# Agent attention and a squared-ReLU FFN: a written order for every engine in the first batch's prologue

## The chip, the core and the metric

The kernel runs on one core of one Trainium2 chip. The metric is device time in microseconds (us); lower is better. The engines are PE (matrix multiplications), PEld (PE's weight loads), DVE (vector), ACT (scalar: activations and copies), POOL (GpSimd) and SP (here it only issues DMAs).

## What is computed

For each of 4 batches there are 12480 tokens of width 128 and 49 agents. In NumPy, with everything in float32 and the two FFN matrices handed over as float64 bits:

```
a2k     = softmax(scale * agents @ k.T)      # 49 x 12480, over the keys
agent_v = a2k @ v                            # 49 x 128
q2a     = softmax(scale * q @ agents.T)      # 12480 x 49, over the agents
x       = q2a @ agent_v                      # tokens x 128
h       = relu(x @ w_in)                     # tokens x 2048
y       = (h * h) @ w_out                    # tokens x 128
```

Since `x @ w_in` is `q2a @ (agent_v @ w_in)`, each batch needs a small table `agent_v @ w_in` (49 x 2048, kept as a high part `aw_hi`, a low part `aw_lo` and a half-precision remainder `aw_ex`), and the FFN multiplies the queries' weights with that table.

## The kernel before

A batch's tokens are cut into 13 blocks of 960; 52 blocks ("groups") of queries in all. The main loop, `first(k)` and `second(k)`, runs 416 pairs: matmuls of the query weights `w`, `x` with the table (tile `h`), a ReLU `r` and a square `g_hi` on ACT, products `gg`, `h` and remainders `g_lo` on DVE and POOL, and matmuls with `wo_hi`, `wo_lo` and `wo_half` into `o`. Keys, values and queries of later batches are slipped between those matmuls. Before the first pair can run, batch 0 needs a prologue, and the change is about that alone:

1. Keys. For each of 13 blocks, 8 matmuls give the scores (`scores`, L243), ACT copies them to `s` (L253), DVE folds them into a running maximum `mx` (L258).
2. `decode_w_in` (L136): `w_in` comes in 8 chunks of 256 columns (`raw`). Per chunk ACT takes the absolute value (L113), DVE clamps and shifts bits (L114, L118, L120, L127, L128), POOL adds the two parts into `win` (L139) and DVE reduces (L140).
3. `maxima` (L261): DVE reduces `mx` over the blocks (L264), PE transposes, DVE reduces again (L272), scales an identity (L274), PE spreads it, and `mb` (L282) holds the maximum of each agent.
4. Values. For each of 13 blocks DVE subtracts `mb` from the scores (L295, `weighed`), ACT takes the exponential (L309), and 8 matmuls (L326, `gathered`) add into the PSUM tile `psa`.
5. Query group 0 (`queries`): matmuls, maximum (L435), difference (L437), exponential, sum (L442), division on POOL (L445), halves (L288, L465).
6. `w_out` comes in 8 chunks too. `most_of_w_out` (L149), `magnitudes` (L114, L118, L120), `powers_of_w_out` (L151 to L171, with one matmul, L163), then `decode_w_out` (L173): DVE L176, L127, L128, ACT L179, L180, POOL L181, L182.
7. `tables` (L348): `x` (L352), matmuls with `quad`, `avT` and `mag` on ACT (L362, L364), a bound and powers of two on DVE, four matmuls with `win`, `aw_hi` on ACT (L402), `aw_lo` on DVE (L404), `aw_half` (L409) and DMAs on SP.

The engines' order here is made by a scheduler which takes what is ready; `issue_after` and `high_priority` push single pieces. So the order in the text of the program isn't the order on an engine. PSUM tiles come from `bank()`: three buffers in rotation (`ps_h`), the same three that the FFN's tiles `h` use.

Of the kernel before, what the change touches and what calls it, by code (L numbers as in the profile page):

```python
# [9 lines left out]
F32 = mybir.dt.float32  # L10
# [19 lines left out]
QAT = 1  # L30
FREE = 4
AFTER = 3
WARM0 = 16
PRE = 12
PAIRED = (0, 2, 4, 6, 1, 3, 5, 7)
OPEN = 10
HELD = 1
# [16 lines left out]
def agent_attention_relu2(ctx: ExitStack, tc: tile.TileContext, qT, kT, v, agT, w_in, w_out, outT):  # L54
# [48 lines left out]
    def load_raw(src):  # L103
        raw = dec.tile([P, WCH, 2], U32, name="raw", bufs=12)
# [4 lines left out]
    def magnitudes(raw, out):  # L109
        high = raw[:, :, 1]  # L110

        t = dec.tile([P, WCH], U32, name="t")
# [4 lines left out]

        nc.vector.tensor_scalar(t, t, 0x07FFFFFF, 3, op0=ALU.bitwise_and, op1=ALU.logical_shift_left)  # L118
        out = t if out is None else out
# [3 lines left out]
        return out  # L123

    def remainders(raw, t):
        rest = dec.tile([P, WCH], F32, name="rest")
        nc.vector.tensor_single_scalar(rest.bitcast(U32), t, 0xFF800000, op=ALU.bitwise_and)  # L127
        nc.vector.scalar_tensor_tensor(  # L128
            out=rest, in0=raw[:, :, 0], scalar=2.0**-52, in1=rest, op0=ALU.mult, op1=ALU.mult
        )  # L130
        return rest
# [4 lines left out]
    def decode_w_in(n, raw):  # L136
        cs = slice(n * WCH, (n + 1) * WCH)
        t = magnitudes(raw, None)
        nc.gpsimd.tensor_add(win[:, cs], t.bitcast(F32), remainders(raw, t))  # L139
        nc.vector.reduce_max(top[:, n : n + 1], win[:, cs], axis=AX.X, apply_absolute_value=True)  # L140

    def load_w_out(n):
        c = slice(n * WCH // C, (n + 1) * WCH // C)
        raw = load_raw(w_out.bitcast(U32).rearrange("(c p) d -> p c d", p=P)[:, c, :])
        return raw

    def most_of_w_out(raws):
        for n, raw in enumerate(raws):
            nc.vector.reduce_max(most_out[:, n : n + 1], raw[:, :, 1].bitcast(F32), axis=AX.X, apply_absolute_value=True)  # L149

    def powers_of_w_out():  # L151
# [10 lines left out]
        ps = ps_t.tile([P, 512], F32, name="o", tag="turn0")  # L162
        last[nc.tensor] = nc.tensor.matmul(ps[:, :1], ones, e.bitcast(F32), start=True, stop=True)  # L163
# [7 lines left out]
        return up.bitcast(F32), down.bitcast(F32)  # L171

    def decode_w_out(n, raw, up):  # L173
        c = slice(n * WCH // C, (n + 1) * WCH // C)
        t = raw[:, :, 1].bitcast(F32)
        nc.vector.tensor_scalar_mul(t, t, up)  # L176
        rest = remainders(raw, raw[:, :, 1])
        hi, lo, half = (x[:, c, :].rearrange("p c d -> p (c d)") for x in (wo_hi, wo_lo, wo_half))
        nc.scalar.copy(hi, t)  # L179
        nc.scalar.copy(half, t)  # L180
        nc.gpsimd.tensor_sub(t, t, hi.bitcast(F32))  # L181
        nc.gpsimd.tensor_add(lo, t, rest)  # L182
# [37 lines left out]
    def spin(n):  # L220
        if alone[0]:
            ps = bank()
            with tc.issue_after(last[nc.tensor].ins):
                for _ in range(n):
                    nc.tensor.matmul(ps[:, :P], ones, ones, start=True, stop=True)
# [35 lines left out]
    def maxima(b):  # L261
# [7 lines left out]
        spin(5)  # L269
# [9 lines left out]
        spin(6)  # L279
        yield 1  # L280
        st["mb"] = small.tile([TP, NA], F32, name="mb")
        st["below"] = nc.vector.tensor_copy(st["mb"], pb[:TP, :NA]).ins  # L282
# [7 lines left out]
    def weighed(b, i, vt, whole, eng):  # L290
        st = state[b]
        s = st["s"][i]
        mb = st["mb"].rearrange("p (o a) -> p o a", o=1).broadcast_to([TP, NT, NA])
        d = s if whole else small.tile([TP, NT, NA], F32, name="d", bufs=2)
        st["less"] = eng.tensor_sub(d, s, mb).ins  # L295
        R, W = (NA, C + 1) if whole else (K2, 2 * (C + 1))
        if not whole:
            vs = kv.tile([TP, NT, W], F32R, name="vs")
            nc.gpsimd.memset(vs.bitcast(F32)[:, :, C : C + 1], 1.0)
            nc.gpsimd.memset(vs.bitcast(F32)[:, :, 2 * C + 1 :], 0.0)  # L300
            nc.scalar.copy(vs[:, :, :C], vt[:, :, :C])
            yield PACE
            last[nc.gpsimd] = nc.gpsimd.tensor_sub(  # L303
                vs[:, :, C + 1 : 2 * C + 1], vt[:, :, :C], vs[:, :, :C].bitcast(F32)
            )
        else:
            nc.scalar.copy(vt[:, :, C:], ones[:TP, :NT].rearrange("p (t o) -> p t o", o=1))
        yield PACE
        nc.scalar.activation(d, d, AF.Exp, scale=scale)  # L309
        if whole:  # L310
            e = d
        else:
            e = small.tile([TP, NT, R], F32R, name="e2", bufs=2)
            yield from halves(e, d, NA, eng)
            vt = vs
        return e, vt, R, W, whole

    def gathered(b, i, e, vt, R, W, whole):
        st = state[b]
        if alone[0]:  # L320
            if i == 0:
                st["av"] = small.tile([K2, 2 * (C + 1)], F32, name="av")
                nc.gpsimd.memset(st["av"], 0.0)
                sums[0] = ps_t.tile([P, 512], F32, name="psa", tag="turn1")
            for t in range(NT):
                nc.tensor.matmul(  # L326
                    sums[0][:R, :W], e[:, t, :], vt[:, t, :],
                    start=(i == 0 and t == 0), stop=(i == NB - 1 and t == NT - 1),
                )
            if i == NB - 1:  # L330
                nc.vector.tensor_copy(st["av"][:NA, : C + 1], sums[0][:NA, : C + 1])
            return
        yield 0
        pv = bank()
        put([
            product(pv[:R, :W], e[:, t, :], vt[:, t, :], start=(t == 0), stop=(t == NT - 1)) for t in range(NT)
        ])
# [496 lines left out]
```

## Time and profile before

| | us |
|---|---|
| median of 3 runs | 1886.37 |
| lowest and highest run | 1885.26, 1886.77 |
| profiled execution, its own time | 1886.58 |
| its span | 1884.8 |
| PE busy | 1864.2 (99%) |
| DVE, ACT, POOL busy | 1646.2, 1667.8, 1334.9 |
| last matmul of the values starts (L326) | 59.93 |
| first matmul of the FFN (L511) | 77.56 |

Times in the trace are counted from the start of the span. PE is busy nearly throughout, except in the first 4% of the span: the page's 40 slices show PE at 9 and 7 tenths in the first two, and at 9 afterwards. A row of a view gives the engine, the line of the program, the tile that is written and the tiles that are read, the shape, and after "x" how many instructions the row holds.

### The profile page before, as it was taken

Reading aid. Unit: us, or ns where it says so; the run is one execution under the profiler, and the core shown is the slowest. Engines: PE = TensorE matmul, PEld = TensorE weight load, DVE = VectorE, ACT = ScalarE, POOL = GpSimd, SP = SyncE. Lnnn points to the kernel's source line nnn. Section 1 sums busy time; section 2 is a strip of 40 time slices with the busy share of each in tenths; the row PEclk is TensorE's granted clock in tenths of the full one; section 3 lists DMA queues with packets and bytes.
Section 4 is the critical chain, followed back from the end, with each engine's and each line's share of the span. In section 5 each row is a group of like instructions: output and inputs, shape, how many; then the busy total and the mean of one; then the engine's idle time right before and its main releaser. Section 6 shows DMA issues by size and latency. Waiting matters only on the chain.

```text
span 1884.8 us, 31149 instructions
## 1 busy us (share of the span) xinstructions
PE 1864.2 (99%) x10848; PEld 1419.0 (75%) x10848; DVE 1646.2 (87%) x1918; ACT 1667.8 (88%) x1607; POOL 1334.9 (71%) x1270
## 2 busy tenths in 40 slices
PE   9799999999999999999999999999999999999999
PEld 9578777777777777777777777777777777777776
DVE  5878888888998898888898888888899989899897
ACT  4578899999888899999888889999988999999997
POOL 1455788887666678888666568898866666767675
PEclk9799999999999999999999999999999999999999
DMA  9233223322112222322212212222112111111110
GB/s 372 75 113 95 80 73 96 93 82 85 54 63 68 84 67 90 95 77 95 78 46 63 81 51 74 82 74 81 58 42 64 41 54 51 52 53 48 52 37 28
DMA packets 74148, 144.53 MB, mean 77 GB/s; under 512 B 9356, under 2 KB 45864, under 8 KB 73992
## 3 DMA queue, kind: packets, MB, share of 16 engines
q1 hardware_dynamic: 73992, 142.55, 23.6%
q8 instruction: 86, 1.41, 0.3%
q14 instruction: 70, 0.57, 0.1%
HBM read 82.89 MB, written 25.56 MB: 58 GB/s over the span
## 4 chain that ended last, share of the span: by engine, by line
PE 93%; DVE 4%; ACT 1%; issue 1%; POOL 1%; POOLq 0%; DVEq 0%; ACTq 0%
PE o L511 56%; PE h L511 26%; PE psa L511 10%; PE h L214 1%; DVE gg L511 1%; ACT r L511 1%; ACT g_hi L511 0%; PE h L670 0%; DVE rest L127 0%; DVE s L295 0%; DVE mx L258 0%; DVE rest L128 0%; DVE g_lo L511 0%; DVE t L114 0%; POOL g_lo L542 0%
## 5 line engine op out<-in xcount | busy, mean ns | idle before, releaser
L542 POOL TENSOR_TENSOR g_lo<-gg,g_hi 128x480 f16<-128x480 f32 x832 | 997.1, 1220 | 454.5 <-ACT g_hi L511 252.9
L511 ACT ACTIVATE r<-h 128x960 f32<-128x960 f32 x832 | 763.6, 968 | 128.4 <-PE h L511 101.1
L511 ACT ACTIVATE g_hi<-r 128x1920 fp32r<-128x1920 f32 x416 | 754.9, 1815 | 26.8 <-POOL g_lo L542 0.4
L511 DVE TENSOR_TENSOR g_lo<-h,g_hi 128x960 f16<-128x960 f32 x416 | 480.0, 1154 | 121.2 <-ACT g_hi L511 93.3
L511 PE MATMUL o<-g_hi,wo_hi 128*128 128x480 f32 x1664 | 570.3, 424 | 0.0
L511 DVE TENSOR_TENSOR gg<-r,h 128x960 f32<-128x960 f32 x416 | 478.7, 1151 | 81.4 <-ACT r L511 72.6
L511 PE MATMUL o<-g_lo,wo_half 128*128 128x480 f16 x1664 | 517.0, 370 | 0.7 <-POOL g_lo L542 0.5
L511 PE MATMUL o<-g_hi,wo_lo 128*128 128x480 f32 x1664 | 496.9, 380 | 0.0
L511 DVE TENSOR_TENSOR h<-r,h 128x960 f32<-128x960 f32 x416 | 480.2, 1154 | 0.7
L511 PE MATMUL h<-w,aw_hi 128*128 128x480 f32 x1664 | 435.0, 383 | 4.5 <-DVE aw_lo L404 2.7
L511 PEld LDWEIGHTS h<-w,aw_hi 128*128 128x128 f32 x1664 | 311.8, 189 | 61.3 <-DVE gg L511 8.7
L511 PEld LDWEIGHTS o<-g_hi,wo_hi 128*128 128x128 f32 x1664 | 315.4, 190 | 48.6 <-issue 3.7
L511 PEld LDWEIGHTS o<-g_hi,wo_lo 128*128 128x128 f32 x1664 | 312.9, 188 | 49.2
L511 PEld LDWEIGHTS <-wo_half 128*128 128x128 f16 x1664 | 167.5, 115 | 124.6 <-issue 92.0
L511 PE MATMUL h<-x,aw_ex 19*128 19x480 f16 x1664 | 159.5, 373 | 0.0
L511 PEld LDWEIGHTS psa<-ag,qt 128*120 128x120 f32 x816 | 140.4, 187 | 18.7 <-DVE ob L511 4.7
L511 PE MATMUL psa<-ag,qt 128*120 128x49 f32 x816 | 126.3, 242 | 0.0
L511 PEld LDWEIGHTS <-aw_ex 19*128 19x128 f16 x1664 | 42.1, 91 | 106.3 <-issue 99.1
L511 PEld LDWEIGHTS psa<-ag,kt 128*120 128x120 f32 x624 | 93.5, 184 | 8.7 <-DVE ob L511 0.6
L511 PE MATMUL psa<-ag,kt 128*120 128x49 f32 x624 | 87.7, 249 | 0.0
L303 POOL TENSOR_TENSOR vs<-vt,vs 120x1024 fp32r<-120x1024 f32 x39 | 85.7, 2198 | 0.0
L511 DVE TENSOR_SCALAR ob<-o,down 128x480 f32<-128x480 f32 x104 | 72.3, 695 | 4.0 <-PE o L511 4.0
(147 smaller groups left out, 1039.6 us busy)
## 6 DMA issues: line engine op xcount, KB each, us to landing
qt<-in_qT SPq DMA_DIRECT2D x52, 480.0 KB
out_T<-ob SPq DMA_DIRECT2D x104, 240.0 KB
vt<-in_v SPq DMA_DIRECT2D x39, 516.0 KB
kt<-in_kT SPq DMA_DIRECT2D x39, 480.0 KB
w<-ph SPq DMA_DIRECT2D x102, 91.9 KB
w<-y SPq DMA_DIRECT2D x102, 91.9 KB
x<-half SPq DMA_DIRECT2D x416, 17.8 KB
ahead<-in_v SPq DMA_DIRECT2D x13, 516.0 KB
```

The lines of the kernel that those rows point to most:

```text
L214: last[nc.tensor] = nc.tensor.matmul(*args, **kw)
L303: last[nc.gpsimd] = nc.gpsimd.tensor_sub(vs[:, :, C + 1 : 2 * C + 1], vt[:, :, :C], vs[:, :, :C].bitcast(F32))
L511: ins = issue(*args, **kw)
L542: chain[nc.gpsimd] = nc.gpsimd.tensor_sub(lo[:, n, :], gg[:, n, :], hi[:, 0, n, :].bitcast(F32)).ins
```

## The change

The prologue is written out anew under `tc.manual_schedule()`: every engine runs its instructions in the order of the program's text. What differs in the work itself:

- The keys' DMAs alternate with those of `w_in`, and `w_in`'s chunks are decoded between the keys. Of a chunk's decode, the product of `rest` with the low word moves from DVE (L128) to ACT (a scaled copy, L135) and POOL (a multiplication, L138).
- The keys' softmax has two parts (`HALF = 7`): blocks 0 to 6 get the maximum `mb`, blocks 7 to 12 the running maximum `mb_late`. The values' sums lie in two PSUM tiles, `psa` and `o`; the first is scaled by `fall` = exp(early maximum less late maximum) when `x` is built (L756, L764).
- The 13 subtractions `s - mb` move from DVE (L295) to POOL (L704).
- One chunk of `w_out` is decoded on DVE behind each of eight blocks of values (L149, L108, L111, L112, L117, L119), and `powers_of_w_out` comes in the second last block; its matmul (L167) stands ahead of the last block's gather. What needs the power of two, `parts_of_w_out`, follows: three instructions on ACT, one on DVE, two on POOL per chunk, four chunks around `tables(0)` and four behind it.
- Two of the 16 small DMAs of the table go out from ACT's queue (L390); idle matmuls (`spin`, 2, 2, 1 and 8) stand between the steps of the table. `raw` has 10 buffers (12), `t` 3 (2).
- The last block of values is loaded twice (L747): 14 loads of values, 13 used.

```
-        t = magnitudes(raw, None)
-        nc.gpsimd.tensor_add(win[:, cs], t.bitcast(F32), remainders(raw, t))
+        t, rest = spare()
+        low = raw[:, :, 0]
+        magnitudes(raw, t, t)
+        nc.scalar.activation(low.bitcast(F32), low, AF.Copy, scale=2.0**-52)
+        nc.vector.tensor_single_scalar(rest, t, 0xFF800000, op=ALU.bitwise_and)
+        yield
+        nc.gpsimd.tensor_mul(low.bitcast(F32), low.bitcast(F32), rest.bitcast(F32))
+        nc.gpsimd.tensor_add(win[:, cs], t.bitcast(F32), raw[:, :, 0].bitcast(F32))
+        yield
         nc.vector.reduce_max(top[:, n : n + 1], win[:, cs], axis=AX.X, apply_absolute_value=True)
...
+        def weigh(i):
+            mb = mbs[i >= HALF].rearrange("p (o a) -> p o a", o=1).broadcast_to([TP, NT, NA])
+            d = st["s"][i]
+            nc.gpsimd.tensor_sub(d, d, mb)
+            nc.scalar.activation(d, d, AF.Exp, scale=scale)
+            nc.scalar.copy(vts[i][:, :, C:], ones[:TP, :NT].rearrange("p (t o) -> p t o", o=1))
...
         for i in range(NB):
+            key(i)
+            more(i)
+            if i == 8:
+                next(early)
+            if i == 10:
+                next(early)
+            if i == 11:
+                next(early, None)
+            for n, delay in ((i - 3, 0), (i - 4, 0), (i - 6, 0)):
+                if 0 <= n < NW:
+                    next(whole[n], None)
...
         for i in range(NB):
+            if i + 1 < NB:
+                weigh(i + 1)
+            gather(i)
+            if i == 0:
+                vts.append(load_values(0, NB - 1, pre, "ahead"))
+            if i < 3:
+                next(late, None)
+            if 1 <= i < NB - 2:
+                ahead_of(q0, 1)
+            n = i - 1 if i < 7 else i - 2
+            if 0 <= n < NW and i != 7:
+                decode_w_out(n, outs[n])
+            if i == HALF + 1:
+                nc.vector.tensor_scalar_mul(x[:NA, :], sums[0][:NA, : C + 1], fall)
+            if i == NB - 3:
+                next(powers)
+            if i == NB - 2:
+                run(powers)
         run(q0)
+        ahead = queries(1)
+        next(ahead)
+        nc.vector.tensor_add(x[:NA, :], x[:NA, :], sums[1][:NA, : C + 1])
+        for n in range(2):
+            parts_of_w_out(n, outs[n])
+        spin(2)
+        made = tables(0)
+        for at, _ in enumerate(made):
+            if at in (1, 3):
+                spin(2 - at // 2)
+            if at in (2, 4):
+                parts_of_w_out(1 + at // 2, outs[1 + at // 2])
+        spin(8)
+        for n in range(4, NW):
+            parts_of_w_out(n, outs[n])
```

DVE among the keys. Before, it had the running maximum of the blocks first (L258), and then two chunks of `w_in` mixed with one another:

```order
L256 COPY mx<-h 120x392
L258 TENSOR_TENSOR mx<-mx,h 120x392 x7
L114 TENSOR_SCALAR t<-t 128x256
L118 TENSOR_SCALAR t<-t 128x256
L114 TENSOR_SCALAR t<-t 128x256
L120 SCALAR_TENSOR_TENSOR t<-raw,t 128x256
L118 TENSOR_SCALAR t<-t 128x256
```

After the change, DVE in the midst of the keys (the late maximum's start, the reduction of the early one, and a chunk):

```order
L141 TENSOR_REDUCE top<-win 128x1
L679 TENSOR_TENSOR mx_late<-s,h 120x392
L683 TENSOR_REDUCE m_360<-mx 120x49
L108 TENSOR_SCALAR t<-t 128x256
L111 TENSOR_SCALAR t<-t 128x256
L112 SCALAR_TENSOR_TENSOR t<-raw,t 128x256
L136 TENSOR_SCALAR t<-t 128x256
```

All eight chunks of `w_in` now stand among the keys (four did before), one behind each maximum; L128 is gone from DVE.

POOL between the keys and the table, after the change (before, POOL had none of the subtractions here, only L139, L445, L288 and L465):

```order
L138 TENSOR_TENSOR raw<-raw,t 128x256
L139 TENSOR_TENSOR win<-t,raw 128x256
L704 TENSOR_TENSOR s<-s,mb 120x392
L740 MEMSET x 98x129
L704 TENSOR_TENSOR s<-s,mb 120x392 x3
L423 TENSOR_TENSOR e<-e,z 120x392
L704 TENSOR_TENSOR s<-s,mb 120x392 x2
L290 TENSOR_TENSOR pp<-e,pp 120x8x49
```

The subtraction of block 0 stands behind the last addition into `win`, and that of block 4 behind the queries' division L423.

PE at the end of the values, before:

```order
L326 MATMUL psa<-ahead,s 49x129 x38
L163 MATMUL o<-e_out,ones 128x1
L326 MATMUL psa<-ahead,s 49x129 x8
L214 MATMUL h<-quad,x 128x98
L214 MATMUL h<-x,quad 98x1
```

and after:

```order
L713 MATMUL o<-ahead,s 49x129 x24
L167 MATMUL h<-e_out,ones 128x1
L713 MATMUL o<-ahead,s 49x129 x8
L229 MATMUL h<-ones 128x128 x2
L219 MATMUL h<-quad,x 128x98
```

The matmul for the power of two stands ahead of the last gather in both. On DVE, the decode that it waits for was spread in pairs of chunks before; after the change each chunk is a row of dependent instructions, and after the powers comes `x` at once, with no decode between:

```order
L149 TENSOR_REDUCE most_out<-raw 128x1
L108 TENSOR_SCALAR t<-t 128x256
L111 TENSOR_SCALAR t<-t 128x256
L112 SCALAR_TENSOR_TENSOR raw<-raw,t 128x256
L117 TENSOR_SCALAR t<-raw 128x256
L119 SCALAR_TENSOR_TENSOR raw<-raw,t 128x256
L156 TENSOR_REDUCE v_out<-most_out 128x1
```

From the first pair of the FFN on, the order of all engines is that of before, but for the two copies of `tables` that changed places in batches 1 to 3.

## Rows read from the trace of the kernel before

**Rows 1.** The page: the span, and busy time of each engine.

```profile
span 1884.8 us, 31149 instructions
PE 1864.2 (99%) x10848; PEld 1419.0 (75%) x10848; DVE 1646.2 (87%) x1918; ACT 1667.8 (88%) x1607; POOL 1334.9 (71%) x1270
```

**Rows 2.** Busy time by stage: window, length, PE, PEld, DVE, ACT, POOL, PEclk, DMA, GB/s.

```profile
7.27:35.44 28.17, 26.79 (x250) 26.26 (x249) 17.05 (x45) 9.68 (x25) 3.02 (x4) 1.00 1.04 399
35.44:60.20 24.76, 24.71 (x218) 23.93 (x218) 23.83 (x80) 12.71 (x35) 6.09 (x8) 1.00 0.67 234
```

**Rows 3.** Timeline of PE: start, us, engine, line, out<-in, count [idle before <-releaser].

```profile
7.10 21.94 PE L214 MATMUL h<-ag,ahead 128*120 128x49 f32 x208
...
35.44 13.05 PE L326 MATMUL psa<-ahead,s 120*49 120x129 f32 x116 [0.28 <-ACT s L309]
...
58.23 1.97 PE L326 MATMUL psa<-ahead,s 120*49 120x129 f32 x16
63.80 0.46 PE L214 MATMUL h<-quad,x 98*128 98x98 f32 x2 [3.60 <-DVE x L352]
```

**Rows 4.** Groups by line and shape, 0 to 80 us, DVE: busy us, mean ns | idle before.

```profile
L258 DVE TENSOR_TENSOR mx<-mx,h 120x392 f32<-120x392 f32 x12 | 6.7, 561 | 7.8 <-ACT s L253 7.8
...
L120 DVE SCALAR_TENSOR_TENSOR t<-raw,t 128x256 uint32<-128x256 uint32 x8 | 3.2, 415 | 0.0
...
L127 DVE TENSOR_SCALAR rest<-t 128x256 uint32<-128x256 uint32 x8 | 2.2, 286 | 0.0
...
L264 DVE TENSOR_REDUCE m<-mx 120x49 f32<-120x392 f32 x1 | 0.8, 802 | 0.0
```

**Rows 5.** Every instruction of L295 in all batches: duration ns min/median/max.

```profile
L295 POOL TENSOR_TENSOR d<-s,mb x39: 943/962/979, 221.1 to 1346.9; 120x392 f32<-120x392 f32 x39
L295 DVE TENSOR_TENSOR s<-s,mb x13: 556/558/560, 34.3 to 40.9; 120x392 f32<-120x392 f32 x13
```

**Rows 6.** Groups by line and shape, 0 to 80 us, POOL and ACT.

```profile
L139 POOL TENSOR_TENSOR win<-t,rest 128x256 f32<-128x256 f32 x8 | 6.1, 763 | 29.1 <-DVE rest L128 29.1
...
L445 POOL TENSOR_TENSOR e<-e,z 120x392 f32<-120x392 f32 x1 | 0.8, 842 | 11.1 <-DVE z L444 11.1
...
L309 ACT ACTIVATE s<-s 120x392 f32<-120x392 f32 x13 | 6.4, 528 | 2.0 <-DVE s L295 2.0
...
L179 ACT CAST wo_hi<-raw 128x256 fp32r<-128x256 f32 x8 | 3.4, 427 | 1.1 <-DVE raw L176 1.1
```

**Rows 7.** Timelines around 26 us and around 46 us, DVE and POOL.

```profile
25.55 0.72 POOL L139 TENSOR_TENSOR win<-t,rest 128x256 f32<-128x256 f32 x1 [0.36 <-DVE rest L128]
...
25.73 0.70 DVE L114 TENSOR_SCALAR t<-t 128x256 f32<-128x256 f32 x1
...
26.46 0.29 DVE L118 TENSOR_SCALAR t<-t 128x256 uint32<-128x256 uint32 x1
...
46.06 1.00 POOL L288 TENSOR_TENSOR pp<-e,pp 120x392 fp32r<-120x392 f32 x1
...
46.17 0.41 DVE L140 TENSOR_REDUCE top<-win 128x1 f32<-128x256 f32 x1
...
46.50 0.71 DVE L118 TENSOR_SCALAR t<-t 128x256 uint32<-128x256 uint32 x1
```

**Rows 8.** Timelines of ACT and DVE from 66 us on.

```profile
72.09 0.69 ACT L402 ACTIVATE aw_hi<-h,rl 98x512 fp32r<-98x512 f32 x1 [6.07 <-DVE down L391]
...
94.77 1.83 ACT L511 ACTIVATE r<-h 128x960 f32<-128x960 f32 x2 [0.74 <-PE h L511]
...
72.81 0.74 DVE L404 SCALAR_TENSOR_TENSOR aw_lo<-h,rl,aw_hi 49x512 fp32r<-49x512 f32 x1 [0.41 <-ACT aw_hi L402]
```

**Rows 9.** Stages of the tail with PE's granted clock (the columns of rows 2).

```profile
60.20:63.80 3.60, 0.01 (x1) 0.00 (x0) 3.60 (x15) 3.32 (x11) 1.11 (x1) 1.00 0.04 14
64.20:74.40 10.20, 5.94 (x13) 2.82 (x12) 6.82 (x19) 3.20 (x9) 9.02 (x12) 0.50 0.00 0
...
77.80:91.50 13.70, 12.57 (x46) 7.44 (x46) 10.79 (x16) 8.84 (x9) 5.08 (x5) 0.50 0.25 73
```

More of the change, by code (lines that the diff above doesn't have):

```diff
@@ L143, in load_w_out, with decode_w_out @@
         c = slice(n * WCH // C, (n + 1) * WCH // C)
[L144 to L149, printed above, removed]
+        return load_raw(w_out.bitcast(U32).rearrange("(c p) d -> p c d", p=P)[:, c, :])
+    def decode_w_out(n, raw):
+        high = raw[:, :, 1]
+        nc.vector.reduce_max(most_out[:, n : n + 1], high.bitcast(F32), axis=AX.X, apply_absolute_value=True)
+        t, rest = spare()
+        magnitudes(raw, t, high)
+        remainders(raw, rest, high)
     def powers_of_w_out():
@@ L161, in powers_of_w_out @@
         )
-        ps = ps_t.tile([P, 512], F32, name="o", tag="turn0")
-        last[nc.tensor] = nc.tensor.matmul(ps[:, :1], ones, e.bitcast(F32), start=True, stop=True)
+        yield
+        ps = bank()
+        nc.tensor.matmul(ps[:, :1], ones, e.bitcast(F32), start=True, stop=True)
         nc.vector.tensor_scalar(v, ps[:, :1], 2.0**-100, 2.0**100, op0=ALU.max, op1=ALU.min)
@@ L222, in spin @@
             ps = bank()
-            with tc.issue_after(last[nc.tensor].ins):
-                for _ in range(n):
-                    nc.tensor.matmul(ps[:, :P], ones, ones, start=True, stop=True)
+            for _ in range(n):
+                nc.tensor.matmul(ps[:, :P], ones, ones, start=True, stop=True)
     state = {}
@@ L288, in halves, with weighed @@
         last[eng] = eng.tensor_sub(out[:, :, n:], x, out[:, :, :n].bitcast(F32))
-    def weighed(b, i, vt, whole, eng):
+    def weighed(b, i, vt):
         st = state[b]
-        s = st["s"][i]
+        d = small.tile([TP, NT, NA], F32, name="d", bufs=2)
         mb = st["mb"].rearrange("p (o a) -> p o a", o=1).broadcast_to([TP, NT, NA])
[L294 to L307, printed above, removed]
+        nc.gpsimd.tensor_sub(d, st["s"][i], mb)
+        vs = kv.tile([TP, NT, 2 * (C + 1)], F32R, name="vs")
+        nc.gpsimd.memset(vs.bitcast(F32)[:, :, C : C + 1], 1.0)
+        nc.gpsimd.memset(vs.bitcast(F32)[:, :, 2 * C + 1 :], 0.0)
+        nc.scalar.copy(vs[:, :, :C], vt[:, :, :C])
+        yield PACE
+        nc.gpsimd.tensor_sub(vs[:, :, C + 1 : 2 * C + 1], vt[:, :, :C], vs[:, :, :C].bitcast(F32))
@@ L308, in weighed @@
         yield PACE
         nc.scalar.activation(d, d, AF.Exp, scale=scale)
[L310 to L318, printed above, removed]
-        st = state[b]
[L320 to L332, printed above, removed]
+        e = small.tile([TP, NT, K2], F32R, name="e2", bufs=2)
@@ L333, in gathered @@
+        yield from halves(e, d, NA, nc.gpsimd)
+        return e, vs
+    def gathered(b, i, e, vs):
+        st = state[b]
         yield 0
[L334 to L337, printed above, removed]
+        pv = bank()[:K2, : 2 * (C + 1)]
+        put([product(pv, e[:, t, :], vs[:, t, :], start=(t == 0), stop=(t == NT - 1)) for t in range(NT)])
         yield 1
@@ L413, in tables @@
             for t in range(NQ):
-                last[nc.sync] = nc.sync.dma_start(ex[t * 32 : t * 32 + NL, n, :], half[SP:, t * P : (t + 1) * P])
+                out, cut = ex[t * 32 : t * 32 + NL, n, :], half[SP:, t * P : (t + 1) * P]
+                if alone[0] and n == 0 and t % 2:
+                    nc.scalar.dma_start(out, cut)
+                else:
+                    last[nc.sync] = nc.sync.dma_start(out, cut)
     qp.tile([P, 8], F32, name="gap", bufs=1)
@@ L622, in rest @@
         vt = load_values(b, 1, kv, "vt")
-        ready = yield from weighed(b, 0, kt, False, nc.gpsimd)
+        ready = yield from weighed(b, 0, kt)
         yield 4
```

208 lines of the change are left out of this document (110 added, 98 removed).

## The prediction

> **What bounds the kernel now.** I read the page first, then a table of busy time by stage, then PE's timeline, then groups by line, and last the timelines of DVE and POOL side by side. PE is busy 1864.2 of 1884.8 us [rows 1]: the FFN is PE's, and the change leaves it as it is. So the change moves the time by as much as it moves the FFN's first pairs, and I count up to the fourth ReLU on ACT, which starts at 94.77 [rows 8]; behind it both kernels run the same order with PE full. Of that stretch the reader should see three parts. Among the keys, 7.27 to 35.44, PE works 26.79 of 28.17 us and DVE only 17.05; among the values, 35.44 to 60.20, PE is full (24.71 of 24.76) and DVE nearly as full (23.83) [rows 2]. So keys have room on DVE, values have none. From the last gather's end (60.20) to the first `aw_lo` (72.81) PE mostly waits: 3.60 us for `x` [rows 3], and ACT 6.07 us ahead of `aw_hi` [rows 8], because DVE's decode of `w_out` stands between the steps of the table.
>
> **What sets the price of a DVE instruction.** `t` at L114 takes 0.70 us when it starts in POOL's L139, and the like instruction L118 0.29 us right after; L118 at 46.50 takes 0.71 beside L288. The reduction at 46.17, beside the same L288, keeps its 0.41 [rows 7]. L258, which reads PSUM, is as steady (mean 561 ns) [rows 4]. So a decode instruction that meets a POOL one is held up by up to 0.42 us in these rows, and reductions and maxima from PSUM are not. The change puts 16 POOL instructions among the keys where 4 were, and 13 among the values, 9 of them subtractions of 0.962 each and the others L423 (842 ns before), the halves and two casts, before e_out is ready [rows 5, 6].
>
> The Trainium skill says so more sharply ("SBUF — State Buffer", section "SBUF: two separate sides"): DVE's fast forms, or those with two SBUF inputs, and GpSimd's share one pair of ports as an exclusive lock, which the first to start keeps for its whole instruction. By that rule the values cost at least the plain sum of what excludes one another, 8 x 1.7 on DVE and 11.8 on POOL (nine subtractions and four others of 0.7 to 1.0), 25.4 us, which is 67.4 for the end of the decode, where my sum by rows comes to 67.7; the trace agrees with it as far as its held-up rows go.
>
> **Keys.** Removed: L128 on DVE. Added: L135 on ACT (nearest row 427 ns for a 128x256 cast [rows 6]; ACT works 9.68 of 28.17 us here [rows 2], so it is covered) and L138 on POOL (as L139, some 0.73). A chunk on DVE is L108 0.29, L111 0.29, L112 0.415, L136 0.286 [rows 4, 7], with 0.03 between dependent ones 1.41. DVE starts decoding at about 15.0, behind the fourth key (7.10 plus 4 x 1.68, plus copy and maximum; 21.94 us are 13 blocks [rows 3]). Until the last L136 it has 8 x 1.41, six maxima x 0.48 (they overlap by 0.08), four reductions x 0.33, and the early maximum's 0.80 plus 0.5: 16.8, so 31.8. Then POOL's two at 0.73, the subtraction 0.96 and an exponential 0.53 [rows 5, 6]: the first gather at 34.5 if nothing is held up. Between both ends, 0 and 16 x 0.42 = 6.7, I take 3.0: POOL runs while DVE has a reduction and a maximum (0.8 of POOL's 1.46 per chunk), so about 0.4 per chunk is left. **First gather 37.5 (34.5 to 41.2), before 35.44.** The memory side has cover: 13 key blocks and 8 chunks come at the 399 GB/s of [rows 2], in some 21 us.
>
> **Values.** Thirteen gathers take 1.80 each (13.05 us for 116 records of 8 a block [rows 3]). The late maximum's two small matmuls stand behind gathers 0 and 1, so DVE gets to `w_out` at 37.5 + 3.6 + 0.9 = 42.0. A chunk is a reduction 0.41, then 0.29, 0.29, 0.415, 0.286, 0.415, with gaps 2.15; eight make 17.2. Beside them `z` 0.9, `fall` and `x` 0.5, the powers' four 0.6: 2.0. Unhindered, the powers are ready at 61.2. The 13 POOL instructions hold it up by between 0 and 0.65 each; I take 0.5, since a subtraction is longer than the rows' 0.72 and 1.00 on average and 80% of what DVE does here can be held: 6.5. So **e_out at 67.7**. PE has twelve gathers done by some 63.1 (37.5 + 12 x 1.80 + transposes 0.9 + 2.3 of waiting for the fourth subtraction, which stands behind L423, which waits for `z`, which stands behind a chunk on DVE). So PE waits 4.6 us for e_out, in front of the last gather. **Last gather ends 69.9, before 60.2: 9.7 later.** Without any hold-up: 61.6.
>
> **Table.** What the change removes here is the decode between the steps, some 8 us of the 12.6. Left on PE and DVE are `x` 0.28, four small matmuls of 0.3 to 0.5, `mag` 0.25, nine small DVE instructions of 0.15, `aw_hi` 0.69, about 4.4 us. On ACT twelve instructions of `parts_of_w_out` at 0.43 stand ahead of the first `aw_hi` (5.2 us from 68.7, with `mag` and `avT` 0.5): 74.4 and thus no later than the chain by 0.2. Each of the two new ACT-queue DMAs is bounded by nothing and by 0.6, twice; ACT is not late there. At full clock aw_lo starts at 74.3. But PE's clock: behind 3.60 us in which PE did 0.01 us of work the granted clock went from 1.00 to 0.50 (1.2 for 2.4 GHz) until 74.4 [rows 9]. Here it waits 4.6 us, so the last gather and the table's matmuls are likely to run at half, which gives 77.5; the five idle matmuls between the steps speak for less. I take 76.5, nearer to the row of half clock. **aw_lo at 76.5 (74.3 to 77.5), before 72.81: 3.7 later.**
>
> **From there to the fourth ReLU.** Before, 94.77 - 72.81 = 22.0, with PE at half clock from 77.80 to 91.50 [rows 9]. After: the eight idle matmuls take a PSUM buffer, so the first pair waits for the table's fourth quarter, one quarter more than before (some 1.2); the ReLU stands behind eleven ACT instructions, and POOL's remainders behind eight additions (1.5 in all); a clock that is back sooner gives 2 back. 22.8, that is 0.8 later (-1 to +3).
>
> **The sum.** 3.7 + 0.8 = 4.5 us on the profiled execution's 1886.58, which stands 0.2 above the median of 1886.37: **1891.0** against the median. The second load of v12 is one more 516 KB transfer, in a stretch where DMA is at 0.67 [rows 2]: nothing, or its 1.4 us if a gather waited for it, and none does. A measurement of this kernel can tell about 0.2%, 3.8 us, from no change: 1882.6 and 1890.1 bound "same".
>
> **The rivals.**
> *POOL and DVE hardly meet.* The subtractions fall into DVE's reductions and its waits, and all hold-ups are near nothing. For it: reductions are 19% of a chunk, and DVE waits for ACT's absolute values now and then. Then gathers end at 61.6, aw_lo starts at 66.1 at full clock (PE does not wait, so the clock has no reason to fall), and the fourth ReLU at 87.8: 7 earlier, 1879.5; with half clock 4 earlier, 1882.5. Against it: the three held-up rows of rows 7, in a stretch where POOL did 6.09 of 24.76 us; now it does some 12. It decides below about 0.15 us of hold-up per POOL instruction. Chance 0.28.
> *In between.* Half of my hold-ups (0.25 among the values, 1.5 us among the keys) at full clock: gathers end at 65.2, aw_lo at 70.0, ReLU 92.8: 2 earlier, 1884.4; or my hold-ups and full clock throughout, 2.3 later, 1888.7. Chance 0.27, within 0.2%; in it is also a small chance that the chip's starts of DMAs or of ACT's table eat what the written order gives.
> *Worse than forecast.* Hold-ups at their upper ends (41.2 for the first gather, 0.65 each) and half clock on: aw_lo near 82, 1895 to 1898. Chance 0.1, counted with the slower ones.
> That the written order isn't kept can be left out: the rows of the engines' order show every piece where the text has it.
>
> **How the numbers follow.** Forecast and the worse case 0.45, slower by over 0.2%; 0.27 within; 0.28 faster. The forecast's own range is 1889 to 1894.5. The range over all cases goes from the end of the first rival's better half, 1880.0, to 1896.0.
>
> **What would show it.** In the profile after: first gather at 37.5, L119 and L117 well above 0.42 and 0.29 in the mean, L704 at 0.96; a wait of PE of some 4 us ahead of L167; the last gather's end near 70; `aw_hi` with no wait on `down` of 6 us; granted clock at half between 66 and 77. The prediction is wrong if L108 to L119 keep their 0.29 and 0.42 beside L704, if the last gather ends before 64, or if the time moves by something behind 100 us, where I say nothing changes.

## The result, and the profile after

The changed kernel takes 1900.69 us (median of 4 runs, 1899.43 to 1901.12) where the kernel before took 1886.15 beside it: a ratio of 1.0076, 95% interval [1.0059, 1.0094]. It is slower by 14.5 us where 4.5 were forecast, and above the range, which ended at 1896.0. The sign was right, but four stretches took longer than forecast. Milestones of the two profiled executions (1886.58 and 1899.43 us), in us from the span's start:

| | before | forecast | after |
|---|---|---|---|
| first gather starts | 35.44 | 37.5 | 42.89 |
| DVE starts on w_out for good | | 42.0 | 49.03 |
| matmul for the power of two (e_out) | 57.92 | 67.7 | 76.77 |
| last gather ends | 60.20 | 69.9 | 80.66 |
| first aw_lo | 72.81 | 76.5 | 85.47 |
| fourth ReLU | 94.77 | 99.3 | 110.93 |

Rows that the table rests on (the kernel before, then two of the change):

```profile
57.92 0.38 PE L163 MATMUL o<-e_out,ones 128*128 128x1 f32 x2
...
49.03 0.41 DVE L149 TENSOR_REDUCE most_out<-raw 128x1 f32<-128x256 f32 x1
...
110.93 1.83 ACT L489 ACTIVATE r<-h 128x960 f32<-128x960 f32 x2 [1.12 <-PE h L489]
```

The fourth ReLU is 16.2 later; the spans differ by 12.8. Some 3 us are won back over the 416 pairs of the FFN in steps of at most 0.5, which I don't explain (the square of the last pair is 13.1 later); the runs' medians say 14.5.

The page, to be read beside [rows 1]:

```profile
span 1897.6 us, 31195 instructions
PE 1875.4 (99%) x10855; PEld 1431.4 (75%) x10855; DVE 1652.3 (87%) x1901; ACT 1675.9 (88%) x1624; POOL 1351.9 (71%) x1291
```

The stages of the change, in the columns of [rows 2]: keys in two windows, values, last gather and table, start of the FFN.

```profile
6.60:18.50 11.90, 11.88 (x114) 11.76 (x112) 5.42 (x12) 4.91 (x12) 1.69 (x2) 1.00 1.03 389
19.50:42.90 23.40, 23.36 (x116) 23.12 (x116) 18.65 (x42) 7.33 (x21) 15.15 (x19) 0.50 1.05 386
42.90:76.80 33.90, 27.13 (x205) 25.05 (x204) 29.08 (x64) 11.08 (x33) 11.60 (x13) 0.90 0.35 115
76.80:85.50 8.70, 8.07 (x41) 6.37 (x42) 4.35 (x20) 6.56 (x15) 4.35 (x7) 0.80 0.01 3
85.50:110.90 25.40, 19.78 (x86) 13.63 (x85) 18.36 (x26) 18.38 (x25) 12.85 (x16) 0.73 0.33 113
```

The second row is the surprise: among the keys PE is busy for 23.36 of 23.40 us at a granted clock of 0.50 (1.2 for 2.4 GHz). Before, the same matmuls ran at 1.00 throughout [rows 2]. PE's timeline of the change shows where it began:

```profile
6.62 11.86 PE L671 MATMUL h<-ag,ahead 128*120 128x49 f32 x112
19.54 13.01 PE L671 MATMUL h<-ag,ahead 128*120 128x49 f32 x64 [1.05 <-DMA ahead<-in_kT]
...
42.89 3.51 PE L713 MATMUL psa<-ahead,s 120*49 120x129 f32 x16
...
54.85 5.40 PE L713 MATMUL psa<-ahead,s 120*49 120x129 f32 x32 [2.31 <-ACT ahead L706]
...
76.77 0.58 PE L167 MATMUL h<-e_out,ones 128*128 128x1 f32 x2 [4.47 <-DVE e_out L162]
77.28 3.38 PE L713 MATMUL o<-ahead,s 120*49 120x129 f32 x16
```

Seven key blocks take 1.69 us each; then PE waits 1.05 us for the eighth block's DMA, which stands behind chunks of w_in on the same queue, and every block after it takes 3.25 to 3.43. The waits of 2.31 (fifth gather) and 4.47 us (e_out) have the forecast lengths, to 0.2 us.

DVE beside POOL, among the keys (first two rows POOL, then DVE):

```profile
18.88 0.84 POOL L138 TENSOR_TENSOR raw<-raw,t 128x256 f32<-128x256 f32 x1 [1.08 <-ACT raw L135]
19.80 0.83 POOL L139 TENSOR_TENSOR win<-t,raw 128x256 f32<-128x256 f32 x1
...
19.13 0.75 DVE L108 TENSOR_SCALAR t<-t 128x256 f32<-128x256 f32 x1
19.91 0.88 DVE L111 TENSOR_SCALAR t<-t 128x256 uint32<-128x256 uint32 x1
```

Both POOL instructions hold up one of DVE's, by 0.46 and 0.59. Summed over the 32 decode instructions (time above 0.295 for L108, L111, L136 and 0.43 for L112, their durations elsewhere) that is 5.9 us. Among the values (first two rows POOL, then DVE):

```profile
61.40 0.58 POOL L443 CAST half<-w 49x480 f16<-49x480 f32 x1 [3.04 <-ACT w L441]
61.94 2.75 POOL L704 TENSOR_TENSOR s<-s,mb_late 120x392 f32<-120x392 f32 x3
...
61.45 3.40 DVE L117 TENSOR_SCALAR t<-raw 128x256 uint32<-128x256 uint32 x1
```

One instruction that takes 0.30 alone waits for four of POOL's in a row. In the second chunk of w_out it is otherwise: POOL's instructions abut there too, and DVE gets one in behind each (first two rows POOL, then DVE):

```profile
52.34 0.84 POOL L423 TENSOR_TENSOR e<-e,z 120x392 f32<-120x392 f32 x1 [10.34 <-DVE z L422]
53.14 1.95 POOL L704 TENSOR_TENSOR s<-s,mb 120x392 f32<-120x392 f32 x2
...
52.40 0.94 DVE L108 TENSOR_SCALAR t<-t 128x256 f32<-128x256 f32 x1
53.37 0.92 DVE L111 TENSOR_SCALAR t<-t 128x256 uint32<-128x256 uint32 x1
```

In all, the 40 decode instructions of w_out are held up by 8.9 us.

Behind the table, ACT's waits in the change (76 to 100 us):

```profile
ACT wo_hi L182 <- DVE up_out L172: 6.8, 1, 6.8
ACT aw_hi L376 <- DMA aw_ex<-aw_half: 3.3, 1, 3.3
```

The two table DMAs on ACT's queue need DVE's `aw_half`, which needs the first `aw_hi`; the second `aw_hi` stands behind them.

### The profile page after: what moved, and what is told of

The parts are those of the page before. It is cut to its first block, busy times and chain, and to the rows that moved or that the text cites. A ratio compares the mean times of both kernels' runs of the same rounds, so it can differ in the third digit from the quotient of the medians.

```text
span 1897.6 us, 31195 instructions
## 1 busy us (share of the span) xinstructions
PE 1875.4 (99%) x10855; PEld 1431.4 (75%) x10855; DVE 1652.3 (87%) x1901; ACT 1675.9 (88%) x1624; POOL 1351.9 (71%) x1291
## 4 chain that ended last, share of the span: by engine, by line
PE 93%; DVE 4%; ACT 1%; DMA 1%; issue 1%; POOL 0%; SPq 0%; ACTq 0%; POOLq 0%; DVEq 0%
PE o L489 56%; PE h L489 25%; PE psa L489 10%; PE h L671 1%; DMA ahead<-in_kT 1%; DVE gg L489 1%; ACT r L489 1%; ACT g_hi L489 0%; DVE t L117 0%; DVE raw L112 0%; POOL g_lo L520 0%; PE psa L713 0%; DVE g_lo L489 0%; PE h L219 0%; DVE raw L119 0%
```

## Experiments

My theory from that profile had three causes: hold-ups of DVE by POOL, the half clock among the keys, and ACT's wait for the table DMAs. The rivals were that one of them hides the others. Runs 1 to 7, 9, 10 and 12 to 14 edit the changed kernel; runs 8 and 11 edit the one before. The kernel before, measured beside each of them, took between 1885.28 and 1886.19, and most runs of one kernel lie 1 to 5 us apart, so a difference of a microsecond between two medians says little. The change's profiled execution is the fastest of its four, 1.3 below its median.

**1. Table DMAs back on SP's queue.**

```
-                if alone[0] and n == 0 and t % 2:
-                    nc.scalar.dma_start(out, cut)
-                else:
-                    last[nc.sync] = nc.sync.dma_start(out, cut)
+                last[nc.sync] = nc.sync.dma_start(out, cut)
```

> The changed kernel, with the two table DMAs that it issues from ACT's queue put back on SP's. In its trace ACT sits idle 3.30 us between the first and the second aw_hi, and its queue holds those DMAs, which wait for aw_half on DVE. Theory (the wait in ACT's order holds up three aw_hi): the second aw_hi follows the first within 1 us, the first FFN matmul comes 2.5 to 3.5 us earlier against aw_lo, the time falls from 1900.7 to 1897 to 1898.5. Rival (SP's sixteen small issues are the limit, and ACT only looked idle): aw_lo of the second quarter earlier, but no change of the time beyond 1 us.

Measured: 1897.15 (ratio to before 1.0064 [1.0049, 1.0079]). DVE's timeline of this run:

```profile
85.34 0.74 DVE L378 SCALAR_TENSOR_TENSOR aw_lo<-h,rl,aw_hi 49x512 fp32r<-49x512 f32 x1 [0.43 <-ACT aw_hi L376]
...
86.49 0.73 DVE L378 SCALAR_TENSOR_TENSOR aw_lo<-h,rl,aw_hi 49x512 fp32r<-49x512 f32 x1
...
92.62 1.14 DVE L486 TENSOR_TENSOR gg<-r,h 128x960 f32<-128x960 f32 x1
```

The second aw_lo follows 1.15 us behind the first; in the change it is 3.98:

```profile
85.47 0.74 DVE L378 SCALAR_TENSOR_TENSOR aw_lo<-h,rl,aw_hi 49x512 fp32r<-49x512 f32 x1 [0.27 <-ACT aw_hi L376]
...
89.45 0.74 DVE L378 SCALAR_TENSOR_TENSOR aw_lo<-h,rl,aw_hi 49x512 fp32r<-49x512 f32 x1 [2.60 <-ACT aw_hi L376]
```

ACT's wait is gone and the median is 3.5 us lower (2.7 if each is taken against the kernel before beside it), in the theory's bracket. But the edit also moved the FFN's first product `gg` on DVE, ahead of the fourth `aw_half` and of four scalings of w_out; runs 10 and 12 to 14 part the two, and most of the gain turns out to need that move.

**2, 3, 4. The clock among the keys, and POOL's second instruction.** Run 2 puts four narrow idle matmuls behind key blocks, run 3 leaves out L138, run 4 does both.

```
+            if 6 <= i:
+                for _ in range(4):
+                    nc.tensor.matmul(fillers[:, :P], ones, ones, start=True, stop=True)
...
-        nc.gpsimd.tensor_mul(low.bitcast(F32), low.bitcast(F32), rest.bitcast(F32))
```

> The changed kernel, with four idle matmuls on PE behind each key block from the seventh on. In the trace of the change PE waits 1.05 us for the eighth key block at 18.5, and its granted clock is 0.50 from 19.5 to about 44, so a key block takes 3.25 us where it took 1.68. Theory (half clock makes PE the bound of the keys, above what DVE's hold-ups cost): granted clock 1.00 among the keys, first gather at about 40 where it is 42.89, DVE at w_out at about 45 where it is 49.03, time 1896 to 1897.5. Rival (DVE bounds the keys, PE at half clock only fills its waits): first gather at 42.5 to 43.5, time 1900 to 1902.

Measured: 1902.06, the four runs from 1900.8 to 1912.07, the mean granted clock of the longest 0.984 and of the shortest 0.992. The profiled one is the longest: its clock fell to 0.50 at 18 and stayed there till 59, and the idle matmuls then only lengthened PE's work (first gather at 54.54). So its trace can't decide between the two. The two shortest runs, 1900.80 and 1900.95 at 0.992, show no gain over the change either; where their clock was full, no trace shows.

> The changed kernel without POOL's multiplication of the low word of w_in (L138), so POOL has 8 instructions among the keys where it had 16; this part of the decode is left out. Theory (two causes in the keys, and PE's half clock lies on top): L111 back to 0.30 us, DVE's last reduction of w_in 2.5 to 3.5 us earlier than 37.2, but the first gather still at 42 to 43, since PE's key blocks at half clock end where they did; time 1900 to 1901.5. Rival (DVE's hold-ups alone set the first gather): first gather at 39.5 to 40.5, time 1897 to 1898.5.

Measured: 1898.95, 1.05 under the theory's bracket. Hold-ups among the keys fall from 5.9 to 0.5 us, yet the first gather is at 42.01: PE, at half clock, bounds the keys.

> Both of the two edits before: idle matmuls behind the key blocks, and POOL's multiplication left out. Theory (half clock first, hold-ups second): first gather at 37 to 38, 2.5 to 3 us before the one with idle matmuls alone; time 1893.5 to 1895. Rival (hold-ups alone count): as without the multiplication alone. Rival (clock alone counts): as with the idle matmuls alone.

Measured: 1893.18; first gather at 37.44, as the theory had it, and a time 0.3 under its bracket. Two of ten runs took 1911.6 and 1915.8, at a mean clock of 0.984 and 0.981 where the others had 0.994 or more; the ratio of 1.0061 [1.0031, 1.0090] is of means, with these two in it (1.0042 for the medians). Windows of run 3 and then of run 4, from 19.5 to the first gather:

```profile
19.50:42.00 22.50, 22.50 (x112) 22.23 (x111) 13.77 (x39) 7.17 (x21) 9.15 (x11) 0.50 1.05 387
```

```profile
19.50:37.40 17.90, 17.90 (x166) 17.71 (x164) 14.14 (x40) 7.70 (x22) 9.22 (x11) 1.00 1.05 388
```

DVE's work is nearly the same (13.77 and 14.14 us) and PE is full in both, though run 4 has 54 records more; it is the clock that parts them. As PE is full up to the first gather in run 4, 37.44 is PE's bound there and not DVE's.

**7. A wide idle matmul in place of the narrow ones.**

```
+            if 5 <= i < NB - 1:
+                nc.tensor.matmul(filler, ones, kts[0][:, :512], start=True, stop=True)
```

> The changed kernel with one idle matmul of 512 columns on PE behind the sixth to twelfth key block, where four of 128 columns were tried: about 0.9 us each at either clock, as the table's matmuls with win show. Theory (PE's waits among the keys bring the half clock, and the narrow matmuls of the keys don't bring the full one back): granted clock 1.00 among the keys in most executions, first gather at about 40, DVE at w_out at about 45, time 1896 to 1897.5. Rival (DVE's hold-ups bound the keys whatever the clock): first gather at 42 to 43.5, time 1900 to 1902.

Measured: 1898.16, all four runs within 1.1 us. Two windows, the keys and the table:

```profile
19.50:40.00 20.50, 18.18 (x128) 14.33 (x127) 19.41 (x44) 7.27 (x19) 13.16 (x17) 0.99 1.05 387
74.00:87.00 13.00, 13.00 (x42) 9.17 (x43) 5.44 (x21) 6.62 (x15) 5.32 (x8) 0.50 0.00 1
```

The clock stays, the first gather is at 40.14 and DVE starts on w_out at 46.19: 2.8 us won, still so at e_out (73.92). With the hold-ups unchanged (5.9), 40.14 is where they alone put the first gather; run 4 has 37.44 without most of them, so they cost at least 2.7. The idle matmul is not 0.9 us at either clock, as the expectation has it: four matmuls with win, of the same width, took 3.73 us at 1.00 (in the change) and 6.36 at a mean of 0.57 (in this run's table). In the profiled execution most of the gain is lost again, since the whole table now runs at half clock: aw_lo at 84.82 is 0.65 earlier. The median is 2.5 lower (1.9 against the kernel before beside it), 0.7 above my upper bound.

**5, 9. The subtractions back on DVE; then with ACT's order mended.**

```
-            nc.gpsimd.tensor_sub(d, d, mb)
+            nc.vector.tensor_sub(d, d, mb)
```

> The changed kernel with its 13 subtractions s - mb back on DVE. Between DVE's first instruction for w_out (49.03) and the end of the powers (76.7) the trace of the change holds 8.9 us of hold-ups: five instructions of the second chunk at 0.92 to 1.05, one L117 of 3.40 us beside three subtractions in a row, one L112 of 2.50 beside two. Theory (the subtractions on POOL make most of these, and cost more than they save): hold-ups fall to about 2 us, nine subtractions add 9 x 0.48 = 4.3 us to DVE in that stretch, e_out 2 to 3 us earlier against the first gather, no wait of 2.31 us in front of the fifth gather, time 1897.5 to 1899. Rival (POOL's work lies beside DVE's and the hold-ups have another cause): e_out 4 to 6 us later, time 1904 to 1907.

Measured: 1907.59 (1.0117 [1.0102, 1.0132]), what the rival had and 0.6 more. But this time is in part luck for the rival. At the fourth pair the profiled execution is 3.5 us behind the change's; two steps of 3.8 and 4.0 us come in the FFN, where a DVE instruction that makes `x` for the table of a later batch is held up by POOL, as in run 10 below:

```profile
490.71 2.78 DVE L327 TENSOR_TENSOR x<-av 98x129 f32<-98x129 f32 x1
...
950.76 2.96 DVE L327 TENSOR_TENSOR x<-av 98x129 f32<-98x129 f32 x1
```

The prologue's part is read from its own milestones. e_out is at 82.23, 5.5 later than in the change, as the rival had it, yet the hold-ups did go, from 8.9 to 1.5 us. What came in their place stands among DVE's waits of this run (49 to 82 us):

```profile
DVE t L108 <- ACT t L107: 5.5, 6, 1.1
```

On ACT the absolute value of a chunk stands behind an exponential, which now waits for a subtraction that DVE does behind the chunk before. My theory had left that circle out. Run 9 puts the absolute value first:

```
+            if chunk:
+                spares = abs_of_w_out(outs[n])
             if i + 1 < NB:
                 weigh(i + 1)
             gather(i)
```

> The changed kernel with the subtractions on DVE, as in the run before that took 1907.6, and ACT's absolute value of a chunk of w_out put ahead of the exponential of the next block. In that run DVE's hold-ups had gone from 8.9 to about 2 us, but DVE waited 0.69 to 1.15 us in seven chunks for the absolute value, which stood on ACT behind an exponential that waited for a subtraction behind the chunk before. Theory (that circle between DVE and ACT cost what the hold-ups gave back): no wait for L107 on DVE, e_out 5 to 6.5 us earlier than 82.23, time 1900 to 1903, so the subtractions cost DVE as much in its own time as they cost it on POOL. Rival (the circle was only where another wait showed): e_out within 2 us of 82.23, time 1905 to 1908.

Measured: 1898.86 (1.0071 [1.0058, 1.0084]), 1.1 below the theory's bracket. DVE's waits of this run for the same instruction:

```profile
DVE t L109 <- ACT t L150: 0.2, 1, 0.2
```

The matmul for e_out is at 77.15, 0.4 later than in the change. So up to e_out the move of the 13 subtractions to POOL is worth nothing either way: it takes some 0.5 us each off DVE and gives them back as hold-ups. Behind e_out the kernel without the move is ahead: its last gather ends at 79.43 (80.66 in the change), its fourth square is 2.0 us earlier and its median 1.8 lower. ACT's new order was not tried in the change alone, but there DVE waits for no absolute value; this is its only wait from 49 to 77 us:

```profile
DVE mb_late L695 <- PE h L694: 1.5, 1, 1.5
```

**6. The matmul for e_out behind the last gather.**

```
-            if i == NB - 2:
+            if i == NB - 1:
                 run(powers)
```

> The changed kernel with the matmul for the power of two (L167) behind the last gather, where it stands ahead of it; the last gather then fills the 4.47 us in which PE waits for e_out. Theory (ACT's six instructions of parts_of_w_out ahead of mag are next in line): x 2.5 to 3 us earlier against e_out, but mag and the first aw_hi only 0.3 to 1 us earlier; time 1899.5 to 1900.5. Rival (what x gains reaches the end): first aw_hi 2.5 us earlier, time 1897.5 to 1898.5.

Measured: 1899.12. x starts at 77.97 (80.70), mag at 80.81 (81.63), aw_hi at 85.04 (84.75), with e_out at 77.03 (76.77). Against e_out x gains the 3.0 us of the theory and mag 1.1, as ACT's six parts of w_out are next in line; aw_hi gains nothing, as the table then ran at half clock till 88. The time lies between the two brackets. A gain isn't shown: the median is 1.6 lower, but at the fourth square the profiled execution is 0.75 later than the change's.

**10, 12. Three mends together (runs 1, 6, 7); then the product of the low word back on DVE.**

> The changed kernel with three single edits together: table DMAs on SP's queue (3.5 us alone), a wide idle matmul behind the sixth to twelfth key block (2.5 us alone), the power's matmul behind the last gather (1.6 us alone). Theory (three separate losses on the path): they add up, 1892.5 to 1894. Rival (they hide one another, since ACT's parts of w_out stand ahead of the table): 1895 to 1897.

Measured: 1900.51 (1.0080 [1.0067, 1.0093]); neither. At the fourth square of the FFN the profiled execution is 2.9 us ahead of the change's, where run 1 alone was 5.7 ahead: with the same queue for the DMAs `gg` stands on DVE behind the fourth `aw_half` and the scalings again, as in the change:

```profile
92.08 0.42 DVE L383 CAST aw_half<-aw_lo 49x512 f16<-49x512 f32 x1 [1.77 <-DMA aw_ex<-aw_half]
92.42 1.99 DVE L185 TENSOR_SCALAR raw<-raw,up_out 128x256 f32<-128x256 f32 x4
94.34 1.14 DVE L486 TENSOR_TENSOR gg<-r,h 128x960 f32<-128x960 f32 x1
```

It then loses 4.0 in the middle of the FFN, where a DVE instruction for batch 2's table meets POOL (timelines of DVE and PE):

```profile
940.64 2.97 DVE L327 TENSOR_TENSOR x<-av 98x129 f32<-98x129 f32 x1
```

```profile
944.30 0.59 PE L486 MATMUL psa<-ag,qt 128*120 128x49 f32 x2 [2.14 <-DVE ob L486]
```

In the change the same instruction takes 0.44 and PE doesn't wait:

```profile
943.59 0.44 DVE L327 TENSOR_TENSOR x<-av 98x129 f32<-98x129 f32 x1
```

Here PE waits 2.14 us, and its clock is 0.50 for the next 3. Runs 1, 5 and 14 have the same 2.97 or 2.96 there, and steps of 2.4, 4.0 and 2.4 us. It hangs on when the two engines meet. So the sum of the mends can't be read from the totals; that the whole of the 14.5 us is made of these parts is not shown.

> The three mends, and the product of the low word of w_in back on DVE as in the kernel before, without the copy on ACT (L135) and the multiplication on POOL (L138). DVE gets eight instructions of 0.43 more (3.4 us), POOL loses eight of 0.84 (in the trace of the change L108 and L111 of six chunks are held up by 0.4 to 0.6 each). Theory (two POOL instructions in a row hold up two of DVE's per chunk, one only one): first gather 0.5 to 2 us earlier than with the mends alone, time 1891 to 1893.5. Rival (DVE's own time counts, the hold-ups move elsewhere): first gather 1 to 3 us later, time 1894.5 to 1897.

Measured: 1895.03 (1.0066 [1.0040, 1.0091]). Hold-ups among the keys fall from 5.9 to 1.8, DVE has 8 x 0.46 more of its own; the last key block starts at 35.46 against 35.28. First gather 41.01 against 40.18, because the queries' matmuls ran at half clock. For DVE the move of this product to POOL was even; the lower time is in part that the step at L327 is absent (at the fourth square run 12 is 0.7 behind run 10), and so decides nothing, though it lies in the rival's bracket. One of the seven runs took 1914.4, at a mean clock of 0.981 where the others had 0.992 or more; it is in the ratio.

**13, 14. What costs the time behind aw_lo.** Four scalings of w_out ahead of x, where they stand ahead of gg; in run 14 with SP's queue.

```
+        for n in range(4, NW):
+            low = outs[n][:, :, 0].bitcast(F32)
+            nc.vector.tensor_scalar_mul(low, low, scale_out[0])
         nc.vector.tensor_add(x[:NA, :], x[:NA, :], sums[1][:NA, : C + 1])
```

> The changed kernel with DVE's four scalings of the last w_out chunks (L185) ahead of x, in a wait of 2.71 us, where they stand ahead of the FFN's first product gg; the fourth aw_half stays ahead of gg. In the trace of the change gg starts at 97.29, behind aw_half at 95.03 (which waited 1.75 us for a table DMA) and four scalings of 2.0 us together. Theory (gg's place behind these on DVE is a loss of its own, apart from ACT's wait): gg 1.5 to 2 us earlier against the first aw_lo, time 1898.5 to 1899.5. Rival (gg waits for the ReLU or POOL anyway): gg within 0.5 us, time 1900 to 1901.

> Table DMAs on SP's queue and the four scalings ahead of x; as with the queue alone, this also puts gg ahead of the fourth aw_half on DVE. With the queue alone aw_lo to gg took 7.3 us (11.8 in the change) and the time was 1897.2. Theory (the queue's gain is made of ACT's wait and of that place of gg; the scalings then stand behind gg and cost little): aw_lo to gg 7 to 7.5, time 1896.5 to 1897.5. Rival (the scalings still hold up the next products): time 1894.5 to 1896.

Measured: 1900.03 and 1897.25. Run 13's time is the rival's and its gain at gg, 0.8, lies between the two; run 14 has what its theory had. With the runs of the same queue, in us from the first aw_lo:

| | ACT waits for the DMAs | ahead of gg on DVE | to gg | to the fourth ReLU |
|---|---|---|---|---|
| change | yes | fourth aw_half, scalings | 11.8 | 25.5 |
| run 13 | yes | fourth aw_half | 11.0 | 25.2 |
| runs 10, 12 | no | fourth aw_half, scalings | 11.4, 11.4 | 25.1, 25.4 |
| runs 1, 14 | no | neither | 7.3, 7.3 | 19.9, 19.9 |

In run 13 gg waits 0.68 us for the ReLU, which ACT's wait has made late. So ACT's wait and the rows ahead of gg lie beside one another, and either hides the other: without ACT's wait alone gg gains 0.4 us, without the scalings alone 0.8, without both waits 4.5. Why gg stands ahead in runs 1 and 14 and behind in 10 and 12, with the same edit of the queue, is not shown.

**8, 11. The kernel before, with the table free of decode.** Run 8 lets `decode_w_out` start only behind x, run 11 only behind L392.

```
-        nc.vector.tensor_mul(rl, rl, up[:K2, :].bitcast(F32))
+        st["scaled"] = nc.vector.tensor_mul(rl, rl, up[:K2, :].bitcast(F32)).ins
...
-    with tc.issue_after(opened):
+    with tc.issue_after(state[0]["scaled"]):
         for n in range(NW):
             decode_w_out(n, raws[n], scale_out[0])
```

> The kernel before, with one edit: the decode of w_out that needs the power of two may only start behind x of the table (in place of behind the last subtraction but two). In the trace of before, x waits 3.60 us for DVE. Theory (the change's real gain lies in the table, where no decode stands between the steps): x 3 us earlier, aw_lo 2 to 4 us earlier than 72.81, time 1882 to 1884. Rival (ACT's sixteen casts and DVE's decode only move behind x and hold up mag and bound instead): aw_lo within 1 us of 72.81, time 1885 to 1886.

Measured: 1883.77 (0.9990 [0.9981, 1.0000]), aw_lo at 69.31. Both are what the theory had; the interval just reaches 1.

> The kernel before, with the decode of w_out that needs the power of two behind the last scaling of rl (L392), so that no decode stands between the steps of the table. With the decode behind x it took 1883.8, and aw_lo started at 69.31. Theory (the table is a chain that any decode between its steps lengthens): first aw_lo at 65 to 67, time 1881 to 1883. Rival (the decode is then late for the FFN's first output matmuls, or stands between the later aw_lo): aw_lo as early, but time 1884 to 1887.

Measured: 1883.23 (0.9985 [0.9976, 0.9994]); aw_lo at 67.06, 0.06 outside the bracket:

```profile
60.86 0.29 DVE L352 TENSOR_TENSOR x<-av 98x129 f32<-98x129 f32 x1
...
67.06 0.73 DVE L404 SCALAR_TENSOR_TENSOR aw_lo<-h,rl,aw_hi 49x512 fp32r<-49x512 f32 x1
...
77.35 1.14 DVE L511 TENSOR_TENSOR gg<-r,h 128x960 f32<-128x960 f32 x1
```

This is the gain that the change has in its table, taken alone: 3.0 us below the kernel before, with an interval below 1. From aw_lo on it gives 2.1 of its 5.8 us back, 10.3 us to gg where the kernel before took 8.2 (72.81 to 80.99), since the decode now stands between the later aw_lo.

## Why the prediction was right and wrong, point by point

- **What bounds the kernel** was right: PE in the FFN, DVE in the prologue, and the change moves the time as it moves the first pairs.
- **Keys** failed twice. First gather 42.89, not 37.5. I took 3.0 us of hold-ups between 0 and 6.7, reasoning that a reduction and a maximum of DVE cover POOL; the trace has 5.9, because POOL's second instruction meets L111 when DVE is back at the decode. That is 2.9 too little. The other 2.75 (run 7) are the half clock, which the step has no term for: it checked that the DMA's total fits ("cover") and not that each block comes in time, so PE's wait at 18.5 was missed, and the half clock that follows it. The floor of 34.5 (34.75 by its own terms) isn't shown by any run; the earliest first gather, run 4's, is at 37.44.
- **Values** were mis-sized: e_out at 76.77, 33.9 us behind the first gather where I had 30.2. DVE begins on w_out 6.1 us behind the first gather and not 4.5, as the first gather still ran at half clock (3.51 us for 1.80). Hold-ups are 8.9 us and not 6.5: the bound of 0.65 for each was no bound, since an instruction can wait for several of POOL's in a row (3.40 and 2.50 us). By the Trainium skill ("SBUF — State Buffer", section "SBUF: two separate sides") an instruction waits out the other engine's whole instruction. The measured 27.7 us, with reductions, z and the powers in it, is not below the least sum of 25.4 that the prediction drew from it, and the trace adds that the wait can go on over the next ones.
- **The wait for e_out** of 4.6 us (4.47), that of the fifth gather (2.3; 2.31) and the table's shortening were right. The fifth gather's wait has the forecast cause. The length of the other is luck: my terms put the twelve gathers' end at 62.3 and not at 63.1, which makes 5.4, and both ends of the wait came 9 us later. (The 1.80 for a gather is 16 records, not the 8 that I wrote.) The last gather, at half clock, took 3.4 us, so that 3.9 passed from e_out to its end where I had 2.2. The table took 4.8 us, which is nearer to my chain at full clock (4.4) than to the 6.6 I took: PE was full from 76.8 on, with the last gather and then the idle matmuls, and at 1.00 again by 81.
- **From aw_lo to the fourth ReLU** I had 22.8; it took 25.5. Two steps failed together. One is the price of the two DMAs on ACT's queue, "bounded by nothing and by 0.6, twice": no run shows the 0.6, and I priced their issue and not `aw_half`, which they wait for; ACT waited 3.3 us. The other is DVE's order, for which the sum has no term: gg stands behind the fourth aw_half, which waits 1.75 us for a table DMA, and four scalings of 2.0 us together. With one of the two mended the stretch takes 25.1 to 25.4 us, with both 19.9 (runs 1 and 14), 2.9 less than my sum, so its other terms were too large by that.
- **The sum**: against the forecast's milestones the keys took 5.4 us more, the values 3.7, the last gather 1.7, the table 1.8 less and the stretch behind it 2.7 more, 11.6 in all at the fourth ReLU. That nothing changes behind 100 us was wrong too: there the change wins 3 us back, and runs 1, 5, 10 and 14 lose 2.4 to 7.7.
- **The rivals**: "POOL and DVE hardly meet" and "in between" are refuted by the hold-ups of both stages; "worse than forecast" had two of the causes but too low a ceiling. That the second load of v12 costs nothing wasn't tried.

## What to carry to other kernels

Before moving work from DVE to POOL, look where DVE's own instructions fall: in these runs 13 subtractions and 8 products changed engines for nothing up to the milestone behind them, since DVE lost as hold-ups what it saved. When an order is written by hand, price every wait by what stands behind it on its queue, a DMA's inputs too, and look for a second wait beside it, which can hide all that a mend gives; and check that each transfer arrives in time, not only that their sum fits: here one wait of PE of 1.05 us was followed by half the clock for the rest of the keys. The gain here lay in one place, the table's chain, and two edited lines of the old kernel take 3.0 us without the rest.

## What the runs showed of the hardware that I had not expected

- PE's granted clock can stay at 0.50 while PE is full: 23.36 of 23.40 us of 49-column matmuls, after a wait of 1.05 us (of 0.25 in run 3, 0.37 in run 2); in the kernel before the same matmuls kept 1.00 with no such wait. It came back among the 129-column gathers in the change, and did not fall before 39 us when a 512-column matmul stood behind the sixth to twelfth block (run 7). Four idle matmuls of 128 columns per block went with 1.00 in the profiled execution of run 4, where PE had no wait, and with 0.50 for 40 us in that of run 2. No run takes the wait alone away, so that it is what brings the clock down isn't shown.
- A DVE instruction that has been held up by one POOL instruction is not always let in before the next: 3.40 us for one of 0.30, with four of POOL's back to back, and 2.97 for one of 0.44 in the FFN (runs 1, 5, 10, 14). Between POOL instructions with a gap of 0.08 us, as among the keys, it was let in, and so it was without a gap in the second chunk of w_out. In the 16 kept traces 27 DVE instructions took over 2 us; each of them began beside POOL's cast to half precision (`half`), with more of POOL's right behind it. Met 0.30 us after its start, that cast held L327 for 2.78 us in run 5; met 0.29 us after, it let L327 in at 0.44 in the change. Whether the cast is the reason, no run shows.
